# Start of the second expert layer: weights in quarters, residues on GpSimd in halves with a small write behind each

## The chip, the cores and the metric

The kernel runs on one core of one Trainium2 chip. The metric is the device time of one execution in microseconds, as the median of several runs. The engines are named as in the profile: PE is TensorE (matrix products), PEld its weight loads, DVE is VectorE, ACT is ScalarE, POOL is GpSimd, SP is SyncE, whose queue issues most of the DMAs.

## The reference

Three layers follow each other: windowed attention, a mixture of experts with a softmax gate (layer 1), and a second mixture of experts with capacity (layer 2), which this change is about. N = 3072 tokens, D = 512, E = 8 experts, F = 1024.

```python
def _moe2_ref(x, w_gate, w1, w2):
    cap = N // E                                  # 384 tokens for each expert
    logits = x @ w_gate
    order = np.argsort(-logits.flatten())
    for idx in order:                             # greedy: best (token, expert) pair first
        tok, e = idx // E, idx % E
        if assigned[tok] >= 0 or counts[e] >= cap:
            continue
        assigned[tok] = e; counts[e] += 1
    for e in range(E):
        mask = assigned == e
        out[mask] = np.maximum(x[mask] @ w1[e], 0.0) @ w2[e]
```

## The kernel before

**Layer 2 runs expert by expert.** `Ffn.run` walks through 64 steps, 8 chunks of 128 hidden columns for each of the 8 experts. Step s multiplies the first matrix of chunk s (12 matmuls into `ph`, L1013), and then the second matrix of chunk s - LAG (9 matmuls into `y0` to `y2`, L937), with LAG = 2. Every float32 product is made of three: each operand is split into a rounded part h and a residue l, and hh, hl and lh are summed. So each chunk of weights needs two steps of preparation: ACT writes the rounded part (`w1h` L904, `w2h` L886) and another engine subtracts it from the raw weights, which gives the residue (`w1l` L909, `w2l` L890). The same is done to the tokens (`xh`, `xl`) and to the hidden values (`hh` on ACT L1023, `hl` on DVE L1024). The first matrix is split LEAD = 3 steps ahead of its step. The second matrix is split LEAD + LAG = 5 steps ahead of its use (`w2at`). Residues of the first matrix go to DVE for even chunks and to POOL for odd ones, those of the second all to POOL, each as one instruction of 128 x 512.

**Weights** come from HBM in halves of an expert's matrix (`load_half`, 1 MB, two buffers for each matrix). Which expert comes k-th is known only at run time, so SP first loads the number from `em` (written by DVE) or, for the second half, from a copy of it: `em2` for the first expert, copied by DVE in `idle(1)`, and `em3` for the others, copied by POOL behind the gathers.

**Routing** replaces the greedy loop. `Route.steps` finds, for each expert in turn, the threshold at which 384 tokens are at or above it: DVE compares all scores with 64 candidates (`cmp`), PE counts with 13 small matmuls into `rt` (L1658), DVE turns the counts into a flag (`gsm`, `gg`), one matmul spreads it (L1941), and after 3 or 4 such rounds the tokens of the expert are marked in `A`. `compact_steps` turns `A` into three lists of 128 token numbers: it ranks the marked tokens (matmuls L1468, L1473, L1474 and the copy `tb`), builds one-hot rows (`ohb`, `ft` on DVE), multiplies them (28 small matmuls, L1500) and writes `idx`. Then POOL issues three indirect DMAs that gather the tokens into `xg` (L1856), PE transposes them (L788, for the first expert L801) and the next expert can start. The results are written with three indirect DMAs of POOL for each expert (L2018), a `drain` behind the third.

**Order.** Nothing is scheduled by a compiler here (`manual_schedule`): each engine executes what the Python code emits, in that order. `side(q)` is called four times in a step: 0 emits the rounded part of w2, 1 its residue, 2 the rounded part of w1, 3 its residue; between them `src.pop()` and `hook` emit a piece of routing when a simple clock model (`clk`) says that its input is ready. Before the first step of layer 2 there is a stretch with no big matmuls, the first chain: the last rows of layer 1, the routing of the first expert, its weights and its gather. PE is fed with idle products there (`wz` into `y0`, L813), `WT` and `IDLE` say how many, and how many pieces of routing go into the three gaps.

## Time and profile before

| what | value |
|---|---|
| median of 3 runs | 874.37 us (871.49 to 876.87) |
| the profiled execution | 876.25 us, its span 874.5 us |
| PE busy | 831.7 us, 95% of the span |
| DVE, ACT, POOL busy | 610.2, 386.0, 350.4 us |
| layer 2, its first `ph` matmul to the end | from 524.89 us of the span |

The span is the profiled time from the first instruction to the last; 1.75 us of that execution's time lie outside it. Times in rows count from the start of the span. PE is close to full on the whole, so what can be won lies where it waits, where its clock is granted at half, or in work that it need not do.

### The profile page before, as it was taken

What the parts mean: (1) busy time and instruction counts of PE and PEld (TensorE: products, weight loads), DVE (VectorE), ACT (ScalarE), POOL (GpSimd) and SP (SyncE); (2) the same over time, 40 slices, a digit from 0 to 9 for tenths busy, and PEclk for the clock granted to TensorE, in tenths of its full rate; (3) what the DMA queues carried; (4) which work ended last, traced back from release to release, by engine and by line L of the source; (5) the groups of instructions that cost most, each with busy time, mean ns of one, the idle gap of its engine ahead of it and who ended that gap; (6) DMA issues with size and microseconds to landing.
All of it is one profiled execution on the core that took longest, in us unless ns stands there. A gap on an engine that the chain in (4) does not pass through costs nothing.

```text
span 874.5 us, 15223 instructions
## 1 busy us (share of the span) xinstructions
PE 831.7 (95%) x5035; PEld 661.7 (76%) x5040; DVE 610.2 (70%) x1759; ACT 386.0 (44%) x1091; POOL 350.4 (40%) x561
## 2 busy tenths in 40 slices
PE   8889999989999999999999979899999998999996
PEld 4666666667888888888887647787888877789995
DVE  6888787766779696969692587577878585763310
ACT  5667777764443434343423124243434342445431
POOL 5456967654221001010000026436464654475561
PEclk9999999999999999999999979999999999999999
DMA  7434645747354435353349045434433443245201
GB/s 209 162 115 140 147 145 147 243 149 210 95 169 134 156 121 169 120 169 119 123 112 321 13 133 170 157 96 128 174 132 134 133 134 131 91 155 190 97 37 40
DMA packets 70109, 122.85 MB, mean 140 GB/s; under 512 B 9857, under 2 KB 23043, under 8 KB 69894
## 3 DMA queue, kind: packets, MB, share of 16 engines
q1 hardware_dynamic: 63302, 102.36, 37.1%
q0 software_dynamic: 6720, 19.43, 6.9%
q8 instruction: 42, 0.69, 0.3%
q14 instruction: 45, 0.37, 0.2%
HBM read 102.06 MB, written 19.71 MB: 139 GB/s over the span
## 4 chain that ended last, share of the span: by engine, by line
PE 75%; DVE 11%; issue 5%; ACT 4%; DMA 2%; POOL 1%; SPq 0%; POOLq 0%; DVEq 0%; ACTq 0%
PE ph L1013 26%; PE y L937 26%; PE sp L322 4%; PE po L394 3%; ACT P L351 3%; PE tr L788 2%; PE rt L1658 2%; PE pt L359 2%; DVE sc L144 2%; PE px L430 1%; PE rc L1500 1%; PE y L813 1%; PE ph L1285 1%; DVE cmp L144 1%; DVE mx L341 1%
## 5 line engine op out<-in xcount | busy, mean ns | idle before, releaser
L1023 ACT ACTIVATE hh<-ph 128x384 fp32r<-128x384 f32 (+1 forms) x112 | 60.2, 538 | 275.2 <-PE ph L1013 274.6
L1013 PE MATMUL ph<-xh,w1h 128*128 128x384 f32 (+1 forms) x448 | 169.5, 378 | 0.0
L1013 PE MATMUL ph<-xh,w1l 128*128 128x384 f32 (+1 forms) x448 | 162.5, 363 | 1.2 <-DVE w1l L909 1.2
L1013 PE MATMUL ph<-xl,w1h 128*128 128x384 f32 (+1 forms) x448 | 162.0, 363 | 0.0
L937 PE MATMUL y<-w2h,hh 128*128 128x512 f32 x384 | 155.9, 406 | 0.0
L937 PE MATMUL y<-w2l,hh 128*128 128x512 f32 x384 | 151.9, 396 | 0.0
L937 PE MATMUL y<-w2h,hl 128*128 128x512 f32 x384 | 151.9, 395 | 0.0
L1024 DVE SCALAR_TENSOR_TENSOR hl<-ph,hh 128x384 fp32r<-128x384 f32 (+1 forms) x112 | 68.5, 611 | 107.1 <-ACT hh L1023 106.0
L890 POOL TENSOR_TENSOR w2l<-w2r,w2h 128x512 fp32r<-128x512 f32 x64 | 86.4, 1356 | 70.5 <-ACT w2h L886 34.8
L1178 POOL DMA_INDIRECT xg<-xd,ent x26 | 28.7, 1104 | 195.4 <-DMA ent<-idtab 149.6
L1202 DVE SCALAR_TENSOR_TENSOR junk<-yr,wgb 128x512 f32<-128x512 f32 x160 | 103.0, 684 | 0.0
L1013 PEld LDWEIGHTS ph<-xh,w1l 128*128 128x128 f32 x448 | 85.4, 191 | 11.1 <-DVE w1l L909 1.6
L1013 PEld LDWEIGHTS ph<-xh,w1h 128*128 128x128 f32 x448 | 85.7, 191 | 10.1 <-DVE hl L1024 0.2
L351 ACT ACTIVATE P<-sp,mx 128x132 f32<-128x132 f32 x192 | 69.3, 369 | 50.8 <-DVE mx L341 17.5
L1013 PEld LDWEIGHTS ph<-xl,w1h 128*128 128x128 f32 x448 | 85.1, 190 | 7.9 <-DVE xl L804 0.3
L937 PEld LDWEIGHTS y<-w2h,hl 128*128 128x128 f32 x384 | 73.0, 190 | 16.1
L937 PEld LDWEIGHTS y<-w2h,hh 128*128 128x128 f32 x384 | 73.4, 191 | 13.7 <-issue 2.2
L937 PEld LDWEIGHTS y<-w2l,hh 128*128 128x128 f32 x384 | 73.2, 191 | 11.6
L886 ACT ACTIVATE w2h<-w2r 128x512 fp32r<-128x512 f32 x112 | 69.8, 625 | 7.7 <-DMA w2r<-in_w_dram 7.6
L904 ACT ACTIVATE w1h<-w1r 128x512 fp32r<-128x512 f32 x112 | 69.6, 623 | 7.2 <-DMA w1r<-in_w_dram 5.1
L322 PE MATMUL sp<-kr,qs 64*128 64x260 f32 (+1 forms) x384 | 59.0, 406 | 13.2 <-ACT P L351 12.0
L909 DVE TENSOR_TENSOR w1l<-w1r,w1h 128x512 fp32r<-128x512 f32 x80 | 65.9, 824 | 3.0 <-ACT w1h L904 3.0
(391 smaller groups left out, 1398.7 us busy)
## 6 DMA issues: line engine op xcount, KB each, us to landing
w1r<-in_w_dram SPq DMA_DIRECT2D x30, 1024.0 KB, 5.8
w2r<-in_w_dram SPq DMA_DIRECT2D x30, 1024.0 KB, 6.9
vr<-in_v_dram SPq DMA_DIRECT2D x16, 384.0 KB, 4.7
xd<-xb SPq DMA_DIRECT2D x16, 384.0 KB, 3.5
xs<-yr SPq DMA_DIRECT2D x24, 256.0 KB, 6.1
kr<-in_kT_dram SPq DMA_DIRECT2D x15, 396.0 KB, 3.8
qr<-in_qT_dram SPq DMA_DIRECT2D x15, 384.0 KB, 4.2
wgb<-in_wg2T_dram SPq DMA_DIRECT2D x1, 2048.0 KB, 9.2
```

The costliest lines, as they stand in the source:

```text
L322: nc.tensor.matmul(sp[:, hd, c0:260], qs[o:o + 64, 128 * i:128 * i + 128], kr[o:o + 64, k0:k0 + 260 - c0], start=True, stop=True)
L351: nc.scalar.activation(z.P[:, n % 2, hd, :], s.sp[:, hd, 128:260], AF.Exp, bias=s.mx[:, hd:hd + 1], accum_out=z.sm[:, n % 2, hd:hd + 1])
L886: nc.scalar.activation(ch[1][c][0], r[:, q, :], AF.Copy)
L890: eng.tensor_tensor(lo, r[:, q, :], h.bitcast(F32), op=OP.subtract)
L904: nc.scalar.activation(h, v, AF.Copy)
L909: eng.tensor_tensor(lo, v, h.bitcast(F32), op=OP.subtract)
L937: nc.tensor.matmul(o, l, r, start=(first and i == 0), stop=(end and i == 2))
L1013: nc.tensor.matmul(ph, wp[:, c, :], xp_[:, c, 0:NTK], start=(d == 0 and i == 0), stop=(d == 3 and i == len(cut[d]) - 1))
L1023: nc.scalar.activation(hh, ph, AF.Relu)
L1024: nc.vector.scalar_tensor_tensor(hl, ph, 0.0, hh.bitcast(F32), op0=OP.max, op1=OP.subtract)
L1178: self.nc.gpsimd.indirect_dma_start(out=self.xg[j][:, a, :], out_offset=None, in_=self.G.xd[0:k, :], in_offset=bass.IndirectOffsetOnAxis(a ...
L1202: nc.vector.scalar_tensor_tensor(junk, yr[:, 0:DM], 1.0, wgb[:, e, :], op0=OP.mult, op1=OP.mult, accum_out=lg[:, e:e + 1])
```

## The change

1. **First weights in quarters.** For the first expert of layer 2, the first half of each matrix comes as two quarters of 512 KB (`load_quarter`). The second quarters and the second halves are issued after the gathers of the first expert, since SP now reads their expert number from `em3`.
2. **Residues on POOL** are made in two instructions of 256 columns, and behind each stands a MEMSET of one element (`gap`).
3. **First matrix:** of the chunks behind the fourth, all residues are on POOL (before, every second one). DVE keeps chunks 0 and 2.
4. **Second matrix:** from chunk 2 on it is split LAG = 2 steps ahead of its use instead of 5; there are 5 buffers instead of 7.
5. **Ranking:** a scan on DVE (`prefix`) and the row sum that comes with `A` replace two of three ranking matmuls and the copy `tb`; of the one-hot products 26 instead of 28 are left; one reduction replaces a copy and an addition before `idx`, which is now two tiles.
6. **Small things:** the last logits are read from PSUM without a copy; fewer idle products in the first chain; some memsets are made earlier; pieces of routing are emitted in a slightly other order.

```diff
+def load_quarter(nc, pool, w, i, e, k):
+    r = pool.tile([128, 4, 256] if i == 0 else [128, 2, 512], F32, name=("w1q", "w2q")[i])
+    sl = slice(256 * k, 256 * k + 256)
...
-        W2B = LEAD + 2 + (0 if self.vsplit else LAG)
+        W2B = LEAD + 2
...
-            w2at[t - LEAD - (0 if small(c) or self.vsplit else LAG)] = c
+            w2at[t - (LEAD if small(c) or self.vsplit else LAG if c > 1 else LEAD + LAG)] = c
...
+        gap = None if self.vsplit else wk.tile([1, 1], F32, name="gap", bufs=1)
+
+        def residue(eng, o, v, h):
+
+            if eng is nc.vector:
+                eng.tensor_tensor(o, v, h, op=OP.subtract)
+                return
+            n = len(o.shape)
+            for k in range(2):
+                w = slice(256 * k, 256 * k + 256) if n == 2 else slice(2 * k, 2 * k + 2)
+                eng.tensor_tensor(o[:, w], v[:, w], h[:, w], op=OP.subtract)
+                eng.memset(gap, 0.0)
...
-                eng = nc.gpsimd if c % 2 and not self.vsplit else nc.vector
+                eng = nc.gpsimd if (c % 2 or c > 3) and not self.vsplit else nc.vector
...
-            poll_w(1)
+            for i in range(2):
+                if not self.vsplit:
+                    raw[i][0].append(load_quarter(nc, wk, (w1, w2)[i], i, src.ereg2(js[0]), 1))
+                poll_w(1, (i,))
...
-JC, NIT, FEW, IDLE = 64, 4, 2, (2, 2, 1)
+JC, NIT, FEW, IDLE = 64, 4, 2, (3, 2, 1)
...
-    nc.tensor.matmul(cs[:, 0:1], A, o1, start=True, stop=True, skip_group_check=True)
-    tb = p.tile([n, 128], BF, name=tag + "tb", bufs=1)
-    V.tensor_copy(tb, bc(cs[:, 0:1], [n, 128]))
-    warm(wt)
-    yield clk.dve + 0.2
-    nc.tensor.matmul(rk, g.tri, A, start=True, stop=False, skip_group_check=True)
-    nc.tensor.matmul(rk, tb, g.tri[0:n, 0:n], start=False, stop=True, skip_group_check=True)
+    nc.tensor.matmul(bs, g.tri, rs, start=True, stop=True, skip_group_check=True)
...
-    V.scalar_tensor_tensor(r0, rk, 1.0, A, op0=OP.add, op1=OP.mult)
+    V.scalar_tensor_tensor(r0, pre, bs, A, op0=OP.add, op1=OP.mult)
...
+    tiles = [t for t in range(n) if n != NR or t % HR <= HT]
+    for t in tiles:
...
-    V.tensor_copy(pj[:, :, 0:3], dg[:, :, 1])
-    V.scalar_tensor_tensor(pj[:, :, 0:3], dg[:, :, 0], 128.0, pj[:, :, 0:3], op0=OP.mult, op1=OP.add)
+    V.tensor_reduce(pj[:, :, 0:3], acc.rearrange("p (k w a) -> p k a w", w=2, a=3), axis=AX.X, op=OP.add)
...
+def prefix(V, g, p, A, tag):
+
+    n = A.shape[1]
+    t = p.tile([128, n], F32, name=tag + "pre", bufs=3)
+    V.tensor_tensor_scan(t, g.ones[:, 0:n], A, 0.0, op0=OP.mult, op1=OP.add)
+    return t
...
     def ready_e2(self, k):
-        return k == 0 or k in self.em3
+        return k in self.em3
...
-                V.scalar_tensor_tensor(A, S_, lo, oe, op0=OP.is_ge, op1=OP.mult)
+                V.scalar_tensor_tensor(A, S_, lo, oe, op0=OP.is_ge, op1=OP.mult, accum_out=rs)
+                pre = prefix(V, g, p, A, "")
```

What this makes of the engines' programs is seen best at three places. On POOL, in the middle of layer 2, around a gather (`DMA xg` x3) and the copy of the expert's number behind it, before:

```order
L890 TENSOR_TENSOR w2l<-w2r,w2h 128x512
L909 TENSOR_TENSOR w1l<-w1r,w1h 128x512
L890 TENSOR_TENSOR w2l<-w2r,w2h 128x512
L1856 DMA xg_7993<-xs,idx 128x512 x3
L1859 COPY em_7997<-em 1x1
L890 TENSOR_TENSOR w2l<-w2r,w2h 128x512
```

and now, around the gather of the second expert:

```order
L902 TENSOR_TENSOR w2l<-w2r,w2h 128x256
L903 MEMSET gap 1x1
L902 TENSOR_TENSOR w1l<-w1r,w1h 128x256
L903 MEMSET gap 1x1
L902 TENSOR_TENSOR w1l<-w1r,w1h 128x256
L903 MEMSET gap 1x1
L1895 DMA xg_6969<-xs,idx_6965 128x512 x3
L1898 COPY em_6973<-em 1x1
L902 TENSOR_TENSOR w2l<-w2r,w2h 128x256
L903 MEMSET gap 1x1
```

Two residues belong to each step now where one and a half did, and a whole one takes four instructions where it took one.

On SP, from the first load of layer 2's weights on (ISA rows are address work; `em_88` is `em2`, `em_6498` and `em_6961` are `em3`), before:

```order
L768 DMA w1r<-in_w_dram 128x4x512
...
L768 DMA w2r<-in_w_dram 128x4x512
L1831 TENSOR_LOAD em_88
...
L768 DMA w1r<-in_w_dram 128x4x512
...
L768 DMA w2r<-in_w_dram 128x4x512
```

and now:

```order
L767 DMA w1q<-in_w_dram 128x4x256
...
L767 DMA w2q<-in_w_dram 128x2x512
L1870 TENSOR_LOAD em_6498
...
L767 DMA w1q<-in_w_dram 128x4x256
...
L776 DMA w1r<-in_w_dram 128x4x512
...
L767 DMA w2q<-in_w_dram 128x2x512
...
L776 DMA w2r<-in_w_dram 128x4x512
```

The first pair has half the bytes, and everything behind it waits for POOL's copy `em3` in place of DVE's `em2`. (Each of the four later loads has a TENSOR_LOAD of its own ahead of it; one is shown.)

On DVE, in the first steps of the first expert, with the flag `gg` for which PE's next count waits, before:

```order
L1024 SCALAR_TENSOR_TENSOR hl<-ph,hh 128x384 x2
L909 TENSOR_TENSOR w1l<-w1r,w1h 128x512
L144 TENSOR_SCALAR gsm<-rt 64x8
L144 TENSOR_TENSOR gg<-rt,gsm 64x8
L1024 SCALAR_TENSOR_TENSOR hl<-ph,hh 128x384
```

and now:

```order
L1054 SCALAR_TENSOR_TENSOR hl<-ph,hh 128x384
L897 TENSOR_TENSOR w1l<-w1q,w1h 128x512
L1054 SCALAR_TENSOR_TENSOR hl<-ph,hh 128x384
L145 TENSOR_SCALAR gsm<-rt 64x8
L145 TENSOR_TENSOR gg<-rt,gsm 64x8
L1054 SCALAR_TENSOR_TENSOR hl<-ph,hh 128x384
```

The residue ahead of the flag was that of chunk 4 (second half, `w1r`); now it is that of chunk 2 (second quarter, `w1q`), one place earlier, and no residue of w1 stands on DVE behind it.

## Rows read from the trace of the kernel before

**Rows 1.** Engines by stretch; the last three numbers are PEclk, DMA share, GB/s.

```profile
524.80:564.00 39.20, 34.18 (x186) 28.44 (x186) 26.69 (x73) 13.76 (x32) 22.47 (x19) 0.91 0.51 165
...
765.00:851.00 86.00, 86.00 (x462) 77.41 (x462) 33.92 (x55) 38.89 (x78) 55.15 (x56) 1.00 0.36 123
```

**Rows 2.** Waits of PE from 524.8 to 866 us: total, times, longest.

```profile
PE tr L788 <- DMA xg<-xs,idx: 3.5, 4, 1.2
PE tr L788 <- DVE xl L790: 3.3, 3, 1.7
PE rt L1658 <- DVE cmp L144: 2.9, 2, 2.2
PE rt L1941 <- DVE gg L144: 2.1, 1, 2.1
```

**Rows 3.** Stretches of half clock in layer 2, as in rows 1.

```profile
536.40:539.80 3.40, 3.40 (x11) 2.91 (x10) 3.26 (x10) 0.93 (x3) 2.68 (x3) 0.50 0.01 2
```

**Rows 4.** Timeline of the first chain: start, us, engine, instruction [idle before <- releaser].

```profile
511.24 0.19 DVE L144 SCALAR_TENSOR_TENSOR r<-rc,A 128x28 f32<-128x28 f32 x1
...
511.89 0.42 SPq L768 DMA_DIRECT2D w1r<-in_w_dram  x1
...
516.37 0.23 DVE L144 SCALAR_TENSOR_TENSOR idx<-pj 128x3 int32<-128x3 f32 x2
...
520.04 0.95 POOL L1856 DMA_INDIRECT xg<-xs,idx  x1 [0.30 <-issue]
...
523.64 0.33 PE L801 MATMUL tr<-cst,xg 128*128 128x128 f32 x1 [0.56 <-DMA xg<-xs,idx]
```

**Rows 5.** Timeline of the third step of the first expert.

```profile
532.83 0.63 ACT L886 ACTIVATE w2h<-w2r 128x512 fp32r<-128x512 f32 x1 [3.98 <-DMA w2r<-in_w_dram]
...
534.39 0.98 DVE L909 TENSOR_TENSOR w1l<-w1r,w1h 128x512 fp32r<-128x512 f32 x1
...
535.82 0.16 PE L1941 MATMUL rt<-gg,ones 64*128 64x8 bf16 x1 [2.09 <-DVE gg L144]
```

**Rows 6.** The chain of waits at the second expert's one-hot products.

```profile
550.52 1.70 PE rc L1500 x28
```

**Rows 7.** Timeline from the second expert's list to its last transposed block.

```profile
552.73 0.23 DVE L144 SCALAR_TENSOR_TENSOR idx<-pj 128x3 int32<-128x3 f32 x2
...
559.48 0.33 PE L788 MATMUL tr<-cst,xg 128*128 128x128 f32 x1 [1.11 <-DMA xg<-xs,idx]
```

**Rows 8.** DVE forms from 520 to 852 us: xcount, busy us, mean ns, idle before.

```profile
L909 DVE TENSOR_TENSOR w1l<-w1r,w1h 128x512 fp32r<-128x512 f32 x31 | 32.5, 1047 | 2.1 <-ACT w1h L904 2.1
```

**Rows 9.** Timeline of a late DVE residue.

```profile
556.28 2.50 DVE L909 TENSOR_TENSOR w1l<-w1r,w1h 128x512 fp32r<-128x512 f32 x1
```

**Rows 10.** POOL forms of the whole span.

```profile
L890 POOL TENSOR_TENSOR w2l<-w2r,w2h 128x512 fp32r<-128x512 f32 x64 | 86.4, 1356 | 70.5 <-ACT w2h L886 34.8 <-ACT ckm L1933 10.4 <-issue 8.3
...
L404 POOL TENSOR_TENSOR psk<-P,psk 128x16 fp32r<-128x16 f32 x48 | 10.5, 219 | 0.0
...
L2017 POOL MEMSET spacer<- 1x1 f32 x24 | 2.2, 90 | 0.0
```

**Rows 11.** POOL timeline, late experts: a gather, then two scatters.

```profile
790.73 1.00 POOL L1856 DMA_INDIRECT xg<-xs,idx  x1 [0.15 <-issue]
...
794.39 2.56 POOL L890 TENSOR_TENSOR w2l<-w2r,w2h 128x512 fp32r<-128x512 f32 x2
...
803.36 1.02 POOL L2018 DMA_INDIRECT out_dram<-yr,idx  x1 [2.08 <-ACT yr L2016]
...
809.12 1.30 POOL L890 TENSOR_TENSOR w2l<-w2r,w2h 128x512 fp32r<-128x512 f32 x1 [2.15 <-issue]
...
838.25 1.00 POOL L2018 DMA_INDIRECT out_dram<-yr,idx  x1 [2.08 <-ACT yr L2016]
```

**Rows 12.** The chain of waits, one undisturbed step of PE.

```profile
799.64 2.10 PE ph L1013 x12
801.75 2.08 PE y L937 x9
```

More of the change, by code (lines that the diff above doesn't have):

```diff
@@ L853, in load, with poll_w @@
                 e = src.ereg2(alljs[hf // 2]) if hf % 2 else src.ereg(alljs[hf // 2])
-                raw[i][hf] = load_half(nc, self.rawpool, (w1, w2)[i], i, e, hf % 2)
-        def poll_w(n):
+                if hf == 0 and not self.vsplit:
+                    raw[i][hf] = [load_quarter(nc, wk, (w1, w2)[i], i, e, 0)]
+                else:
+                    raw[i][hf] = load_half(nc, self.rawpool, (w1, w2)[i], i, e, hf % 2)
+        def poll_w(n, ws=(0, 1)):
             for _ in range(n):
-                for i in range(2):
+                for i in ws:
                     w = want[i]
@@ L889, in split2 @@
                 eng = nc.vector if self.vsplit or small(c) and c % 2 else nc.gpsimd
-                eng.tensor_tensor(lo, r[:, q, :], h.bitcast(F32), op=OP.subtract)
+                residue(eng, lo, r[q // 2][:, q % 2, :] if isinstance(r, list) else r[:, q, :], h.bitcast(F32))
                 done[1] = c + 1
@@ L896, in split1 @@
                 v = r[:, q, :]
+            elif isinstance(r, list):
+                v = r[q // 2][:, :, 128 * (q % 2):128 * (q % 2) + 128]
             else:
@@ L958, in run @@
             split(-LEAD, 3)
-            ahead = [(s, 2) for s in range(1 - LEAD, 0)] + [(-LEAD, 0), (1 - LEAD, 0)]
+            ahead = [(s, 2) for s in range(1 - LEAD, 0 if self.vsplit else 2 - LEAD)] + [(-LEAD, 0), (1 - LEAD, 0)]
             for s, part in ahead:
@@ L967, in run @@
             for s in range(2 - LEAD, 0):
-                split(s, 0)
-                late.append(s)
+                part = 0 if self.vsplit else 2
+                split(s, part)
+                late.append((s, part + 1))
         clk.pe = max(clk.pe, clk.dve - X0)
@@ L976, in side @@
             def side(q):
+                while q == 3 and late:
+                    split(*late.pop(0))
                 if q == 1 and late:
-                    late.append(s)
+                    late.append((s, 1))
                 else:
                     split(s, q)
-                while q == 3 and late:
-                    split(late.pop(0), 1)
                 if jx + 1 < len(js) and s < total:
@@ L1546, in __init__ @@
         self.cmp = p.tile([128, 2, JC, HR], BF, name="cmp")
+        self.cuts = ((0, HA), (HA, HT + 1))
+        self.cmp2 = [p.tile([128, 2, JC, e - o], BF, name=f"cmp{o}") for o, e in self.cuts]
         self.T = p.tile([128, NR], F32, name="T_")
@@ L1693, in v1 @@
             V.tensor_tensor(Lm, Lm, bc(self.fl[:, None, None, :], [128, 2, HT, E]), op=OP.max)
+            for i in range(SSML):
+                V.tensor_scalar(L[64:128, HR * i + HT], self.fl[64:128], self.pad[64:128, i:i + 1], None, op0=OP.mult)
         def v2():
@@ L2156, in moe2_general @@
             V.copy_predicated(L, mk, neg)
-            idx = compact(nc, g, p, f.ps.tile([128, 512], F32, name="rc"), A, "g")
+            rs = p.tile([128, 1], BF, name="grs")
+            with nc.allow_low_precision("a count of at most NT"):
+                V.tensor_reduce(rs, A, axis=AX.X, op=OP.add)
+            idx = compact(nc, g, p, f.ps.tile([128, 512], F32, name="rc"), A, rs, prefix(V, g, p, A, "g"), "g")[0]
             xg = p.tile([128, 3, DM], F32, name="gxg")
```

93 lines of the change are left out of this document (48 added, 45 removed).

## The prediction

> **What bounds the kernel now.** I read the busy table first: PE is busy for 95% of the span, so only three things can shorten it: PE's waits, stretches at half its clock, and work taken off PE. By stretch [rows 1], 765 to 851 us is full (86.0 of 86.0 us, clock 1.00), while the first expert of layer 2, 524.8 to 564, has 5 us idle and a clock of 0.91. An undisturbed step takes 2.10 + 2.08 us [rows 12], so an expert 33.4 us. 64 steps would be 268 us, but from 524.89 to the last scatter, about 866 us, there are 341: 42.6 for each expert. The list of PE's waits behind 524.8 us [rows 2] holds 11.8 us: 3.5 for gathers, 8.3 for DVE. The clock was granted at 0.50, the lower level (1.2 of 2.4 GHz), in five stretches of 3.3 to 3.4 us with PE busy throughout (one of them is in [rows 3], the others begin at 560.3, 601.2, 717.3 and 734.3); each came just behind PE's waits or a run of small count matmuls, and each costs half its length, 1.7 us, 8.5 together. So at most 20.3 us of layer 2 can be won without removing work. The rest of the difference to 268 us is transposes and routing matmuls, which remain.
>
> **The change part by part.**
>
> *First chain.* The ranking result `r` stands at 511.24 [rows 4]. One small matmul now stands where three and a copy did; against that come a scan and a second accumulator read on DVE. I take 0.6 us off, and 0.3 more for one reduction in place of copy and addition, and for the second `idx` no longer standing ahead of the gather. The list then comes near 515.5 instead of 516.4, the third gather near 519.1 instead of 520.04. The last block landed 3.6 us behind its issue (523.64); that stays, since the 2 MB of weights issued from 511.89 on were not what it waited for. Another 0.2 us come from the logits that aren't copied. Sum: 1.1 us; bounds 0 (DVE's comparison for the second expert falls onto a gather again) and 2.2 (1 MB less traffic helps the gather as well).
>
> *Quarters.* In the third step ACT stood 3.98 us for a half of w2 that was issued 525.26 and landed 532.8; behind it in ACT's order stood `hh` and `w1h`, behind these on DVE a residue at 534.39 and the flag, and PE waited 2.09 us for it [rows 5], then ran 3.4 us at half clock. Now the second pair of loads waits for POOL's copy behind the gathers, near 520 us, instead of DVE's, and the first of them is a quarter, so chunks 2 and 3 should be there near 525 and the halves near 528 and 532, and the residue ahead of the flag is one that needs the quarter alone. On SP nothing but these loads is queued behind the new wait. I take the whole 2.1 us off and the clock stretch with it, 1.7: 3.8. If the quarter is late, the same stall comes back: bound 0.
>
> *PE work.* For each of the seven later experts two small matmuls and two of 28 one-hot products go. The 28 took 1.70 us [rows 6], so two 0.12; a lone small matmul has 0.16 [rows 5]. 7 x (0.12 + 0.32) = 3.1 us as records stand; they overlap, so I take 2.5 and keep 1.5 and 3.1.
>
> *Second expert.* PE waited 2.9 of the 3.5 us here, with the list at 552.73 and the last block transposed at 559.48 [rows 7]. In the new order 9 `ph` matmuls stand behind the one-hot products that stood ahead of them: 1.6 us of work move under the gather. I take 1.0 off the wait and half of the clock stretch behind it: 1.8; bounds 0 and 4.6.
>
> *DVE.* 30 residues leave it. In layer 2 one took 1.05 us on the mean, 31 of them 32.5 us [rows 8], the one at 556.28 2.50 us [rows 9] while POOL ran residues of its own. Others that read two operands from SBUF stretch likewise. DVE's relief costs nothing by itself; it counts where PE waits for it: 3.3 (`xl`) and 2.9 (`cmp`) [rows 2]. I take two thirds, 4.2, and two of the three clock stretches that are left, 3.4. Bounds 0 and 6.2 + 5.1.
>
> A stretched DVE instruction looks like one that stands still until POOL's instruction is over. The Trainium skill (SBUF — State Buffer, Who interferes with whom) says that a DVE instruction with two SBUF inputs contends with a GpSimd instruction that reads SBUF, but not with one that only writes. The trace agrees with the first half (2.50 us for the residue at 556.28); no row here shows the second. By it DVE gets in at the MEMSET behind a half, and the whole 11.3 us of the upper bound would go. If it isn't, a DVE instruction waits for a whole row of halves, and nothing goes.
>
> *POOL.* A residue of 512 columns takes 1.30 us undisturbed [rows 11], a subtraction of 16 columns 0.219, a one-element MEMSET 0.09 [rows 10]. Between the first two a half is 0.219 + 240 x (1.30 - 0.219) / 496 = 0.74 us, so a residue is 2 x (0.74 + 0.09) = 1.66 us; lower bound 1.3 (halves add nothing), upper 2.2 (each half waits some 0.27 us for DVE besides). An expert needs 16 of them, 26.6 us, where it needed 12 and 15.6. The gather holds POOL for 3.7 us (790.73 to 794.39), scatter and drain for 5.8 (803.36 to 809.12) [rows 11]. That is 36.1 us. PE needs 34.9 for a late expert (803.36 to 838.25 [rows 11]) and 40 or more for one with routing. So POOL, half idle before, is nearly full, and just too slow for one late expert. The last one gathers nothing. The second matrix's residue now has two steps, 8.4 us, ahead of its use, instead of five. A scatter and drain of 5.8 us, with the wait for `yr` ahead of it (2.08), takes nearly all of that. I put 1.3 us on this, and 0.5 on fewer idle products ahead of the first step. The gather stands in POOL's queue behind residues that may be late; this is in the bounds of the second expert.
>
> Sum: 1.1 + 3.8 + 2.5 + 1.8 + 4.2 + 3.4 - 1.8 = 15.0 us. Against the profiled execution's 876.25 this is 861.3; that one lies 1.9 us above the median of its three runs, from which the sum gives 859.4. I say 860.
>
> **The rivals.**
>
> *POOL becomes the bound* (slower). Its time for an expert is 16 r + 9.5 us. It reaches the present 42.6 at r = 2.07 and the forecast's 40.7 at r = 1.95. At r = 2.3, if halves mostly wait for DVE, an expert takes 46.3 us and eight 370 instead of 341: 876 + 29 - 7 (first chain, quarters and PE work) = 898; at r = 2.2 it is 885. For it: today's means lie just above the undisturbed time (1356 against 1300 ns [rows 10]) with POOL half idle, and they must rise when it is full. Against: it takes 0.3 us on each residue more than I reckon.
>
> The Trainium skill (GPSIMD Engine Reference, 4.1 Engine selection) says to keep elementwise work on VectorE, GpSimd being about half as fast with two inputs. The trace agrees less strongly, 1.30 us against a mean of 1.05 under contention [rows 8, 11]. By that rule this rival would be the likely case.
>
> *The waits move* (same). The MEMSET lets no DVE instruction in ahead of the next half, or POOL's lateness gives back what DVE gains: 1.1 + 2.1 + 2.5 = 5.7 us remain, less 1.8 for POOL: 872. For it: gathers, DVE and PE wait for each other in turn, and a chain relieved at one end is often held at the next.
>
> *All waits go* (faster). 20.3 + 2.5 + 1.1 = 24 us: 852. For it: DVE has 30 residues less and planned gaps; against: the second expert's gather alone lasts longer than the work laid over it.
>
> **How the numbers follow.** Forecast 0.56, waits move 0.20, all waits go 0.14, POOL bound 0.10. The forecast's own range is 853 to 867. No change means within 1%, 865.6 to 883.1, about what a measurement of this kernel can tell. Faster: 0.14 and nearly all of 0.56, 0.68; same: 0.20 and a rest, 0.23; slower: 0.09. The range leaves out the rival on the slow side and half of the fast one: 850 to 872.
>
> **What would show it.** Right: no wait of PE for the flag in the third step; first `ph` near 523.7; DVE's `ub`, `cmp` and `oc` with no records of more than half a POOL residue above their usual; POOL's busy time in layer 2 near 265 us, halves near 0.75 us. Wrong: PE waiting for `w2l` or `w1l` of POOL at L963 or L1043, above all behind scatters; halves above 0.95 us; half-clock stretches of the same number as now.

## The result, and the profile after

| | median (range), us | against before |
|---|---|---|
| before | 872.88 (867.35 to 876.87), 22 runs | |
| changed | 876.99 (874.89 to 880.91), 22 runs | ratio 1.0055, interval 1.0039 to 1.0072 |

The change makes the kernel 0.55% slower. That is inside the 1% that the prediction called no change, but the interval lies wholly above 1. 860 us was forecast, with 872 as the upper end. The profiled execution has a span of 874.8 us. That of the kernel before, 874.5 us, belongs to an execution 3.4 us above its median, so the two traces end level where the medians differ by 4.1 us.

The first part of the gain arrived. This is the timeline of PE in the changed kernel: start, us, engine, instruction [idle before <- releaser].

```profile
523.21 0.42 PE L1043 MATMUL ph<-xh,w1h 128*128 128x384 f32 x1
...
532.99 0.18 PE L1978 MATMUL rt<-gg,ones 64*128 64x8 bf16 x1
...
609.84 0.34 PE L1043 MATMUL ph<-xh,w1h 128*128 128x384 f32 x1
...
645.97 0.95 PE L1695 MATMUL rt<-OH,cmp 128*128 128x16 bf16 x13 [4.56 <-DVE cmp L145]
...
692.26 0.95 PE L1695 MATMUL rt<-OH,cmp 128*128 128x16 bf16 x13 [5.47 <-DVE cmp L145]
...
705.79 0.33 PE L1043 MATMUL ph<-xh,w1h 128*128 128x384 f32 x1
...
777.95 0.33 PE L1043 MATMUL ph<-xh,w1h 128*128 128x384 f32 x1
```

And this is the same of the kernel before, at the first `ph` of steps 16, 31 and 44 (counted from 0).

```profile
618.99 0.33 PE L1013 MATMUL ph<-xh,w1h 128*128 128x384 f32 x1
...
699.32 0.33 PE L1013 MATMUL ph<-xh,w1h 128*128 128x384 f32 x1
...
777.15 0.34 PE L1013 MATMUL ph<-xh,w1h 128*128 128x384 f32 x1
```

The first step begins at 523.21 instead of 524.89. The flag's matmul at 532.99 comes without the wait of [rows 5]. Step 16 begins at 609.84 instead of 618.99: 9.2 us won. Step 31 begins at 705.79 instead of 699.32: 15.6 us lost in 15 steps. Up to step 44, 5.7 of these are won back (777.95 against 777.15). The two rows between show where the loss is, 4.56 and 5.47 us of idle PE in front of a count. The waits of PE from 524.8 to 866 us are, as in [rows 2] (total, times, longest):

```profile
PE rt L1695 <- DVE cmp L145: 10.0, 2, 5.5
PE tr L796 <- DVE xl L798: 4.4, 3, 2.8
PE rc L2035 <- DVE OH L145: 3.2, 1, 3.2
PE tr L796 <- DMA xg<-xs,idx: 1.5, 2, 0.9
```

PE waits less for gathers (1.5 for 3.5) and hardly for the flag, but 10.0 instead of 2.9 us for `cmp`, and 3.2 for the last check (L2035). By stretch, as in [rows 1], first the lossy one:

```profile
610.00:706.00 96.00, 82.65 (x508) 70.81 (x507) 72.45 (x177) 31.41 (x74) 60.54 (x139) 0.93 0.33 110
...
765.00:851.00 86.00, 86.00 (x461) 77.81 (x460) 16.45 (x34) 39.17 (x79) 69.16 (x177) 1.00 0.42 135
```

The kernel before has hardly any idle PE (80.06 of 80.30 us busy) and no half clock in the same steps, 16 to 31:

```profile
619.00:699.30 80.30, 80.06 (x513) 68.35 (x512) 60.11 (x164) 30.95 (x70) 45.24 (x43) 1.00 0.42 145
```

In and behind the long waits of the changed kernel, the clock was granted at 0.50, the lower of its two levels, in these stretches:

```profile
644.60:651.40 6.80, 5.43 (x28) 5.14 (x29) 2.95 (x8) 1.21 (x3) 0.00 (x0) 0.50 0.02 4
689.00:695.80 6.80, 3.54 (x21) 3.45 (x22) 4.09 (x6) 0.43 (x2) 2.11 (x6) 0.50 0.61 207
743.60:747.00 3.40, 3.40 (x11) 2.91 (x10) 3.30 (x7) 1.70 (x4) 2.54 (x5) 0.50 0.80 301
```

PE was busy for 12.4 us of these 17.0 and idle for the rest, so they cost half of 12.4, 6.2 us, against the 8.5 of the kernel before.

Why `cmp` is late stands on DVE and POOL. The timeline of DVE around the first of the two waits, then at the second:

```profile
637.58 0.18 DVE L145 MAX8 J8m<-rt 128x8 f32<-128x8 f32 x1 [0.90 <-PE rt L1978]
637.79 6.79 DVE L145 SCALAR_TENSOR_TENSOR sc<-J8m,dd,sc 128x1 f32<-128x1 f32 x2
644.50 0.29 DVE L145 TENSOR_SCALAR ub<-S__77,sc,dd 128x28 bf16<-128x28 f32 x1
...
684.54 6.53 DVE L145 TENSOR_SCALAR ub<-S__77,sc,dd 128x28 bf16<-128x28 f32 x1
```

The timeline of POOL over the first:

```profile
637.24 0.72 POOL L902 TENSOR_TENSOR w2l<-w2r,w2h 128x256 fp32r<-128x256 f32 x1
637.91 0.09 POOL L903 MEMSET gap<- 1x1 f32 x1
637.96 0.72 POOL L902 TENSOR_TENSOR w2l<-w2r,w2h 128x256 fp32r<-128x256 f32 x1
...
643.71 0.71 POOL L902 TENSOR_TENSOR w2l<-w2r,w2h 128x256 fp32r<-128x256 f32 x1
644.38 0.09 POOL L903 MEMSET gap<- 1x1 f32 x1
```

Two instructions on 128 single numbers, usually 0.2 us each, take 6.79 us and end with POOL's row of halves (6.66 of it is the first one's). The `ub` at 684.54, usually 0.29 us, takes 6.53. In the first of the two, nine halves and the MEMSETs between them went by. The next half starts 0.05 us after its MEMSET's start (637.96, 637.91), so POOL is never idle between two halves. The halves themselves, as in [rows 10], from 523 to 866 us, are not slow:

```profile
L902 POOL TENSOR_TENSOR w1l<-w1r,w1h 128x256 fp32r<-128x256 f32 x120 | 92.9, 776 | 64.3 <-ACT w1h L930 44.6 <-issue 5.9 <-PE y L963 5.7
L902 POOL TENSOR_TENSOR w2l<-w2r,w2h 128x256 fp32r<-128x256 f32 x120 | 91.0, 759 | 8.7 <-ACT w2h L910 8.6
...
L903 POOL MEMSET gap<- 1x1 f32 x251 | 22.5, 89 | 0.0
```

### The profile page after: what moved, and what is told of

The parts are those of the page before. It is cut to its first block, busy times and chain, and to the rows that moved or that the text cites. A ratio compares the mean times of both kernels' runs of the same rounds, so it can differ in the third digit from the quotient of the medians.

```text
span 874.8 us, 15582 instructions
## 1 busy us (share of the span) xinstructions
PE 820.6 (94%) x5006; PEld 656.5 (75%) x5006; DVE 589.2 (67%) x1730; ACT 385.4 (44%) x1091; POOL 412.1 (47%) x968
## 4 chain that ended last, share of the span: by engine, by line
PE 73%; DVE 16%; ACT 5%; issue 3%; DMA 1%; POOL 1%; DVEq 0%; POOLq 0%; ACTq 0%
PE ph L1043 27%; PE y L963 26%; PE sp L323 4%; PE po L395 3%; ACT P L352 3%; DVE sc L145 2%; PE tr L796 2%; PE rt L1695 2%; PE pt L360 2%; PE rc L1530 1%; DMA xg<-xs,idx 1%; PE px L431 1%; DVE mx L342 1%; DVE cmp L145 1%; DVE ub L145 1%
## 5 line engine op out<-in xcount | busy, mean ns | idle before, releaser
L902 POOL TENSOR_TENSOR w1l<-w1r,w1h 128x256 fp32r<-128x256 f32 x120 | 92.9, 776 | 64.3 <-ACT w1h L930 44.6
L902 POOL TENSOR_TENSOR w2l<-w2r,w2h 128x256 fp32r<-128x256 f32 x120 | 91.0, 759 | 8.7 <-ACT w2h L910 8.6
L323 PE MATMUL sp<-kr,qs 64*128 64x260 f32 (+1 forms) x384 | 59.0, 405 | 13.2 <-ACT P L352 12.0
L930 ACT ACTIVATE w1h<-w1r 128x512 fp32r<-128x512 f32 x108 | 67.4, 624 | 2.3 <-DVE lp L449 2.1
L910 ACT ACTIVATE w2h<-w2r 128x512 fp32r<-128x512 f32 x108 | 67.4, 624 | 0.0
```

Of the source, the lines that this page charges most:

```text
L323: nc.tensor.matmul(sp[:, hd, c0:260], qs[o:o + 64, 128 * i:128 * i + 128], kr[o:o + 64, k0:k0 + 260 - c0], start=True, stop=True)
L902: eng.tensor_tensor(o[:, w], v[:, w], h[:, w], op=OP.subtract)
L910: nc.scalar.activation(ch[1][c][0], r[q // 2][:, q % 2, :] if isinstance(r, list) else r[:, q, :], AF.Copy)
L930: nc.scalar.activation(h, v, AF.Copy)
```

## The experiments

Theory A: the thirty residues moved to POOL make its rows long. Theory B: halves with a tiny write behind each hold DVE, wherever the residues stand. Theory C: the late split of w2 bunches the residues. All edits are to the changed kernel unless another is named; ratios are against before, with their 95% interval. A hold is a record of DVE that is far longer than usual; the lengths given are those of the records. A seam is the place between two instructions of POOL that follow each other.

### Parts of the change undone

**w1_back**

```diff
-                eng = nc.gpsimd if (c % 2 or c > 3) and not self.vsplit else nc.vector
+                eng = nc.gpsimd if c % 2 and not self.vsplit else nc.vector
```

> The changed kernel with the w1 residues divided as before (odd ones on GpSimd, even ones on VectorE); halves, gaps, quarters and first chain stay. Theory A (the thirty residues that moved to GpSimd make its back-to-back rows so long that VectorE, in the middle of routing, is held 6.5 to 6.8 us three times): the rows shorten, no VectorE instruction of layer 2 is held for more than 2.5 us, the idle of PE after 523 us falls from 22 to about 12, the early 9 us stay: 864 to 869 us, ratio to before 0.990 to 0.996. Theory B (halving with a gap is what holds VectorE, wherever the residues stand): the long records stay, VectorE has 20 to 30 us more work besides: 876 to 885. Theory C (the later split of w2 bunches them): 874 to 878, unchanged.

872.38 us, 1.0008 (0.9982 to 1.0033). Two records of `sc` of 6.8 us are still there, with idle PE of 4.7 us behind each, as B said; the time, under B's 876, lies between the two. A alone doesn't explain it. The edit also puts back a charge in the code's clock model, which comes up below.

**whole**

```diff
-            if eng is nc.vector:
+            if eng is nc.vector or len(v.shape) > 0:
                 eng.tensor_tensor(o, v, h, op=OP.subtract)
                 return
```

The condition is always true, so every residue is one instruction, with no write behind it.

> The changed kernel with each residue on GpSimd as one instruction of 512 columns and no gap behind it; the division of the residues, quarters and first chain stay. Theory A (load of GpSimd makes the rows): a residue costs 1.30 to 1.36 us against 2 x 0.76 + gaps, some 0.2 to 0.3 us less, so the rows shorten a little but stay: longest VectorE record 4 to 6 us, 871 to 877 us. Theory B (halves and gaps hold VectorE): the records fall back to the 1.4 to 2.2 us of before and the time to 864 to 869. If the halves do let VectorE in elsewhere, it is over 880.

877.46 us, 1.0054 (1.0027 to 1.0080), with holds of 4.1 to 5.0 us. As A said; B's second half fell: whole residues hold DVE too.

**w1_back_whole**, both edits together.

> The changed kernel with both undone: w1 residues divided as before and whole, no gaps. What is left of the change is the first chain, the quarters and the later split of w2. Theories A and B both: the time before less the 9 us that step 16 shows, 862 to 868 us, ratio 0.988 to 0.995. Theory C (the later split of w2): 870 to 877. If the early 9 us are given back further on by a wait that was there before too, 870 to 873.

870.79 us, 0.9964 (0.9935 to 0.9994). More than A and B said, and within what C, or a gain given back further on, would give. One hold of 5.9 us is left, without a write.

**no_gap**

```diff
-                eng.memset(gap, 0.0)
```

> The changed kernel without the tiny writes; two halves stay for each residue on GpSimd. If a gap lets a waiting VectorE instruction in, the records of VectorE lengthen further (over 7 us) and the time rises above 880. If the gap opens nothing (theory A, the next half starts 0.05 us after the write), GpSimd saves some 0.05 to 0.09 us a half, some 5 us of its busy time in all, the long records of 6 to 7 us stay or get shorter by a tenth, and the time is 874 to 878, no change against the changed kernel.

867.24 us, 0.9946 (0.9918 to 0.9975). 9.8 us less than the changed kernel: neither expectation had it. The same place in the program, timeline of DVE:

```profile
642.10 1.52 DVE L145 SCALAR_TENSOR_TENSOR sc<-J8m,dd,sc 128x1 f32<-128x1 f32 x2
643.55 0.79 DVE L145 TENSOR_SCALAR ub<-S__77,sc,dd 128x28 bf16<-128x28 f32 x1
644.37 1.57 DVE L145 TENSOR_TENSOR cmp<-ub,iou 128x1792 bf16<-128x1792 bf16 x1
```

DVE waits there for the end of a half each time and gets on, though `sc` comes 2.0 us into POOL's row here (from 640.11) as in the changed kernel (from 635.79). Theory D: the write makes DVE lose its turn.

**w1_back_no_gap**, the first edit and this one.

> Halves without the tiny write, and the w1 residues divided as before. It shows what the move of the thirty residues is worth when the write is gone: VectorE has some 30 x 0.85 us of work back, GpSimd 30 x 1.4 us less. Theory D (the write was the fault, the move is good): 868 to 873 us, 1 to 5 us over the 867.2 of the kernel without the write. Theory A (the move was the fault): 861 to 866.

856.80 us, 0.9805 (0.9768 to 0.9841): the fastest kernel of this study, 16 us under before. The move of the residues, too, costs some 10 us.

**w2_earlier_no_gap** (without the write)

```diff
-        W2B = LEAD + 2
+        W2B = LEAD + 2 + (0 if self.vsplit else LAG)
...
-            w2at[t - (LEAD if small(c) or self.vsplit else LAG if c > 1 else LEAD + LAG)] = c
+            w2at[t - (LEAD if small(c) or self.vsplit else LEAD + LAG - 1 if c > 1 else LEAD + LAG)] = c
```

> Halves without the tiny write, and w2's chunks split four steps ahead of their use instead of two (before: five), with two more buffers. Theory C (the later split of w2 puts its residues where they are late): PE's waits for GpSimd's residues and the row behind the gathers shrink, 862 to 866 us. If the later split costs nothing: 866 to 869, as the kernel without the write.

882.02 us, 1.0101 (1.0067 to 1.0135). C fell, and the other way round: the late split is worth 15 us in this order. PE waits 6.4 us for `w1l` of POOL here, and two holds of 6.4 and 5.5 us at `sc` came up, with no write between the halves. So the write isn't needed for a hold.

**wide_gap**

```diff
-        gap = None if self.vsplit else wk.tile([1, 1], F32, name="gap", bufs=1)
+        gap = None if self.vsplit else wk.tile([128, 256], F32, name="gap", bufs=1)
```

> The changed kernel with the write behind each half widened from one element to 128x256. GpSimd has about 250 x 0.1 to 0.3 us = 25 to 75 us more work, still under 500 of 875. If a longer write-only stretch lets VectorE in at every half (which the prediction had of the tiny one), the longest VectorE record on the routing chain falls from 6.7 to under 1.6 us, the three halts of PE of 4.6, 5.5 and 5.4 us and the half clock behind them go: 864 to 869 us, as without the write. If it doesn't, the rows get longer with GpSimd's work: 878 to 890.

899.66 us, 1.0291 (1.0254 to 1.0329). That is above both expectations. Holds of 8.4 and 6.5 us run across writes of 0.30 us each, so a longer write doesn't let DVE in here. GpSimd's own lateness is in this time as well: PE waits 4.6 us for a `w1l` of POOL.

**halves_alone**, the kernel before with the two halves and no write.

```diff
-                eng.tensor_tensor(lo, r[:, q, :], h.bitcast(F32), op=OP.subtract)
+                residue(eng, lo, r[:, q, :], h.bitcast(F32))
...
-                eng.tensor_tensor(lo, v, h.bitcast(F32), op=OP.subtract)
+                residue(eng, lo, v, h.bitcast(F32))
```

> The kernel before, with one edit: each residue on GpSimd is issued as two halves, with no write between them. First chain, loads, the early split of w2 and the division of the residues stay as before. If the halves are what makes the best kernel so far (856.8 us) faster than the same with whole residues (870.8), this takes about as much off the kernel before: 858 to 865 us. If they help only together with the later split of w2 or the quarters, 869 to 874.

874.77 us, 1.0014 (0.9986 to 1.0043): nothing. Halves took 14.0 us off in the new kernel (870.79 to 856.80), but not here, where a DVE residue held for 4.8 us puts a wait of 5.0 in front of the flag's matmul of [rows 5]. That wait was 2.1 before, so it explains only 2.9 us of the 14; the rest stays open.

**quarter_residues**, w1_back_no_gap with four instructions of 128 columns.

> The best kernel so far (no tiny write, w1 residues divided as before, 856.8 us) with each GpSimd residue in four instructions of 128 columns instead of two of 256. If VectorE's wait is the rest of one GpSimd instruction, its usual hold falls from 0.4 to 0.7 us to 0.2 to 0.35, some 10 us of VectorE's time, of which a third to a half stands on the chain: 852 to 856 us. GpSimd's residues cost more, 4 x 0.42 against 2 x 0.73 us. If VectorE misses short seams as it does behind the tiny write, or if GpSimd's time counts: 858 to 870.

873.93 us, 1.0016 (0.9984 to 1.0048), 17 us over the halves and above both expectations: six records of DVE over 2.5 us, the longest of `idx` 11.0 us. Finer isn't better here.

### The order that moved along

In the code stands, beside the choice of the engine, the charge of 0.6 us to the clock model that orders the routing pieces. A residue moved to POOL is not charged, and so routing is emitted earlier.

**no_gap_old_plan** (without the write, residues on POOL)

```diff
-                if eng is nc.vector:
+                if eng is nc.vector or c % 2 == 0:
                     clk.vec(0.6)
```

> Halves without the tiny write, all late w1 residues on GpSimd as in the changed kernel, but the clock by which the code orders the routing steps still adds 0.6 us for each even chunk, as if VectorE did it. Theory F (the move costs 10 us because the order changes: without these 0.6 us the routing's VectorE work is emitted earlier, in front of xl, and TensorE waits 3.4 us for xl): the order is that of the 856.8 us kernel, VectorE has 26 us less to do, and the time is 853 to 860. Theory G (the move costs because GpSimd's queue is full, gathers and residues come later): 864 to 869, as without the write (867.2).

858.42 us, 0.9842 (0.9805 to 0.9879). This is what theory F expected: 8.8 of the 10 us (867.24 to 858.42) come from the order. Without the charge, DVE's timeline in front of expert 4 (no_gap) has the routing ahead of `xl`:

```profile
688.20 0.71 DVE L145 SCALAR_TENSOR_TENSOR sc<-J8m,dd,sc 128x1 f32<-128x1 f32 x1
...
693.19 0.80 DVE L145 TENSOR_TENSOR OH<-L,S__77 128x224 bf16<-128x224 f32 x1
...
695.28 0.55 DVE L798 TENSOR_TENSOR xl<-tr,xh 128x384 fp32r<-128x384 f32 x1
```

and its PE waits for that:

```profile
695.88 0.55 PE L796 MATMUL tr<-cst,xg 128*128 128x128 f32 x3 [3.39 <-DVE xl L798]
```

With the charge (no_gap_old_plan) the two `xl` come first and nobody waits:

```profile
687.25 0.56 DVE L798 TENSOR_TENSOR xl<-tr,xh 128x384 fp32r<-128x384 f32 x1 [1.12 <-ACT xh L797]
...
689.33 0.56 DVE L798 TENSOR_TENSOR xl<-tr,xh 128x384 fp32r<-128x384 f32 x1 [0.47 <-ACT xh L797]
...
690.00 0.32 DVE L145 SCALAR_TENSOR_TENSOR sc<-J8m,dd,sc 128x1 f32<-128x1 f32 x1
```

**w1_back_new_order**, w1_back_no_gap without the charge for chunks behind the fourth.

```diff
-                if eng is nc.vector:
+                if eng is nc.vector and c <= 3:
                     clk.vec(0.6)
```

> The kernel of 856.8 us (no tiny write, w1 residues divided as before), but the clock that orders the routing steps no longer adds 0.6 us for the even late chunks, though VectorE still does them: TensorE's and ScalarE's instructions then stand in the order of the changed kernel, row for row. Theory F (the order costs the 10 us): 866 to 872 us, with TensorE waiting some 3 us for xl and for the last check as without the write (3.4 and 3.1). Theory G (GpSimd's load costs): 855 to 860.

864.42 us, 0.9917 (0.9885 to 0.9950), 7.6 us over the same in the old order, and the wait for `xl` of 3.2 us is back. Somewhat less than F said, but not G.

**tiny_write_old_order**, the changed kernel with the charge of no_gap_old_plan.

> The changed kernel, tiny writes and all, with the one number put back: the clock adds 0.6 us for each even late chunk, so TensorE's instructions stand in the order of before's division. If the write costs the same in every order (9.8 us in the new one, 15.6 with the residues back): 868 to 874 us, with at least two VectorE records of 6 us and more. If the write hurts only where the new order has piled up VectorE's work: 858 to 862.

890.22 us, 1.0215 (1.0185 to 1.0244). Far over both expectations: the write costs 31.8 us here (858.42 without it). With the write in place, the old order alone makes the changed kernel 13.2 us slower, not faster. There are five holds of 4.4 to 11.3 us; PE's waits from 520 to 888 us:

```profile
PE tr L796 <- DVE xl L798: 13.2, 4, 5.0
PE rt L1695 <- DVE cmp L145: 11.0, 3, 5.4
```

**changed_again**, the changed kernel profiled a second time.

> The changed kernel as it is, profiled a second time. If the long holds are bound to places in the program: again sc and ub records of 6 to 7 us in steps 22 and 29 to 30, and PE idle of 4 to 6 us behind them. If they are chance, other places or other lengths, with some 15 to 25 us of PE idle in all since the run's time is steady (874.9 to 880.9).

Holds of 6.7 us at `sc` and 7.3 at `cmp` (usually 1.1), at the same two places of the program (the second one instruction later), and PE idle of 4.58 and 5.47 us behind them (4.56 and 5.47 the first time). In both traces the holds belong to places in the program.

### The holds by themselves

**seams** computes nothing of the reference; in outline:

```python
for r in range(ROW):                 # GpSimd: a row of residues, nothing to wait for
    P.tensor_tensor(lo[:, a], wr[:, a], wh[:, a], op=OP.subtract)   # then, by kind, a write
    P.tensor_tensor(lo[:, b], wr[:, b], wh[:, b], op=OP.subtract)
for it in range(ITER):               # VectorE, with TensorE in between
    V.max(J8, rt[:, 0:8])
    V.scalar_tensor_tensor(sc[:, 0:1], J8[:, 0:1], dd[:, 0:1], sc[:, 1:2], op0=OP.mult, op1=OP.add)
    ...
    V.tensor_tensor(cmp, bc(ub[:, None, :], [128, 64, 28]), bc(iou[:, None, :], [128, 64, 28]), op=OP.is_ge)
```

> A kernel that computes nothing of the reference (all three layers are left out): it measures the disputed cost by itself. In each of 24 phases GpSimd subtracts 24 residues in a row from data that is there already, while VectorE runs nine rounds of the routing step's chain (a maximum out of PSUM, two 128x1 instructions, ub, a comparison of 128x1792, then the count on TensorE). The phases take turns: halves, halves with the tiny write, whole residues, halves with a write of 128x256 behind each, whole ones with the tiny write, VectorE alone. Theory D (the tiny write makes VectorE lose its turn at a seam): with the tiny write some VectorE instructions of 128x1 or 128x28 are held for 3 us and more over several halves, without it none or clearly fewer; the next half starts within 0.06 us of the tiny write. Theory E (the write changes nothing, the three long records of the changed kernel are chance): as many long records with as without. If a write-only stretch lets VectorE in, the phase with the wide write has no record over 1.6 us; if it holds VectorE as a reading one does, long records stand there too.

There is no long hold in any of the 20 rows: the longest wait of a DVE instruction over halves is 0.6 us without the write and 0.8 with it, about the length of one half. The wide writes had been moved out of their place, so that kind said nothing.

**seams_in_order**, the same with the order as written.

> The measurement by itself again, computing nothing of the reference, now with the order on each engine as written (in the run before, the wide writes were moved out of their place), with ScalarE's halves ready before the row and TensorE reading the residues behind it. Thirty phases, six kinds in turn: halves; halves with the tiny write into one element that all share; halves with a tiny write into an element of its own each, so that the write waits for no write before it; halves with the write of 128x256; whole; whole with the tiny write. From the run before: without the write VectorE goes in at the first seam (4 of 95 held instructions missed one), with it 60 of 100 missed one. If the write itself is the fault, its own element changes nothing: over half miss the first seam. If its wait for the write before is the fault, the kind with own elements goes in at the first seam like plain halves. With the wide write: if GpSimd's write-only stretch lets VectorE in, no hold over 0.75 us; if not, as with the tiny one.

| kind (5 rows each) | held over 0.15 us | held on the mean (longest) | from one start to the next |
|---|---|---|---|
| halves | 64 | 0.48 (0.56) us | 0.680 us |
| halves, tiny write | 70 | 0.51 (0.61) | 0.719 |
| halves, tiny write to its own element | 71 | 0.52 (0.61) | 0.719 |
| halves, wide write | 51 | 0.44 (0.82) | 0.933 |
| whole | 47 | 0.96 (1.09) | 1.220 |
| whole, tiny write | 46 | 1.01 (1.13) | 1.257 |

Held is what a record of `sc`, `ub` or `cmp` lasts beyond the shortest of its kind. No wait reaches the time from one start to the next, with the write or without: DVE waits for the rest of one instruction of POOL and gets in. The counts of missed seams in the expectation above (4 of 95 against 60 of 100) don't show otherwise. They hang on 0.04 us: an instruction that starts at a seam stands 0.02 us ahead of the next half in a plain row and 0.06 us behind a write, and then waits for that half in both. If each half that starts during a wait is counted, there are 36 in 64 waits without the write and 39 in 70 with it. So theory D isn't borne out by these rows, and no row of the 30 shows a long hold.

**seams_after_gathers**

> The measurement by itself once more, computing nothing of the reference: each row of 14 residues now follows three gathers of 128 rows and a copy on GpSimd, as in the second layer, and a weight load of 1 MB runs beside it. Kinds: halves, halves with the tiny write, whole; eight phases each. If the gathers make the long holds, VectorE records of 2 us and more stand in the first 10 us behind them; without such records the gathers are not it. The seams should show as before: 3 of 64 missed without the write, over half with it.

All 24 rows held the first 128x1 instruction that came into them to their end, 15.1 to 18.0 us, of each kind alike, with the write or without.

**seams_apart**

> The measurement by itself, computing nothing of the reference, halves without the tiny write only. Seven ways to come into the row, four times each: plain (VectorE's chain starts 2 us behind the row's start), early (it starts with the row), load (plain, with a weight load of 1 MB running), one (plain, one gather ahead of the row), three (three gathers ahead), pause (three gathers, then GpSimd waits some 4 us, then the row), far (the same with a wait of some 15 us). If the gathers make the long holds: plain, early and load get in at the first or second seam (no record over 1 us), one and three hold to the row's end, 14 to 17 us, and pause or far tells whether a rest clears it. If coming late into a running row does it: plain and load hold as well, early does not. If the load does it: load alone.

27 of 28 rows held, plain ones too; the exception is one row behind three gathers. The rows meant to start together with DVE's chain held as well: the first `sc` still came 1.0 us behind the row's start. So it isn't the gathers, the load or a rest. What the rows of the last two runs share is that the first of `sc`, `ub` and `cmp` to meet the row came 1 to 3 us behind its start; in each of the 50 rows of the two runs before, one of them was running when the row began. Later rounds of the chain came into those 50 rows up to 17 us and more behind their start and got in, so coming late is not enough: it is the first meeting with the row that differs.

**seams_breaks**

```diff
                 P.tensor_tensor(lo[:, a], wr[:, a], h[:, a], op=OP.subtract)
+                P.tensor_copy(one[:, 2 * r:2 * r + 1], lo[0:1, e].bitcast(F32))
```

> The measurement by itself, computing nothing of the reference: rows of 28 halves into which VectorE's chain comes 2 to 3 us late, as the rows that held it to their end (16 us). Six kinds, four rows each: plain; a tiny write into an element of its own behind each half; a write of 128x256 behind each half; a one-element copy behind each half that reads the half's last column and so waits until it is done; the same behind each second half; a one-element copy behind each second half that waits for ScalarE to have read the residue. If only an idle GpSimd ends a hold: plain, tiny and wide hold for 14 us and more, the copies that wait let VectorE in within 0.8 us (behind each half) or 1.6 us (behind each second). If the wide write gives way too, the holds of 6 and 8 us in the full kernel with it stay unexplained. If the waits for the own result don't help and the one for ScalarE does, GpSimd's pause has to be longer than some 0.1 us.

The timeline of DVE in a plain row, in one with the wide write and in one with a copy that waits for each half (the edit above):

```profile
14.91 16.23 DVE L154 SCALAR_TENSOR_TENSOR sc<-J8m,dd,sc 128x1 f32<-128x1 f32 x1
...
116.31 0.57 DVE L154 SCALAR_TENSOR_TENSOR sc<-J8m,dd,sc 128x1 f32<-128x1 f32 x1
...
116.94 22.57 DVE L156 TENSOR_SCALAR ub<-S__71,sc,dd 128x28 bf16<-128x28 f32 x1
...
172.82 0.52 DVE L154 SCALAR_TENSOR_TENSOR sc<-J8m,dd,sc 128x1 f32<-128x1 f32 x1
...
173.40 0.88 DVE L156 TENSOR_SCALAR ub<-S__71,sc,dd 128x28 bf16<-128x28 f32 x1
```

Plain, tiny and wide: 12 of 12 rows held an instruction to their end, 16.1 to 22.6 us. The three kinds of copies that wait: none of 12. The timeline of POOL in that last row:

```profile
172.61 0.71 POOL L139 TENSOR_TENSOR lo<-wr,h 128x256 fp32r<-128x256 f32 x1
173.39 0.17 POOL L145 COPY one<-lo 1x1 f32<-1x1 f32 x1
173.53 0.71 POOL L132 TENSOR_TENSOR lo<-wr,h 128x256 fp32r<-128x256 f32 x1
```

The copy starts 0.07 us after the half's end (173.32), while a write starts 0.05 us before it. A half with such a copy takes 0.92 us instead of 0.68. The copies that wait end the holds; that the 0.07 us of rest does it, and not something else about the copy, is argued, not shown. In the full kernel no copy was tried.

## Why the prediction was wrong, point by point

The failed step is the term for DVE: waits less 4.2 us and clock less 3.4. Waits for `cmp`, `xl` and the last check rose from 6.2 to 17.6 us. Of three stretches of half clock, 5.1 us, the term was to remove two; three remained and cost 6.2. The prediction let DVE in at the MEMSET behind a half and named its own alternative: otherwise a DVE instruction waits for a whole row. That is what happened, at two places, 6.7 and 6.5 us long. Two things stand behind the loss. The first is shown by taking it away alone, the second only where the first is gone:

- **The write.** Its removal is worth 9.8 us in the changed kernel (876.99 to 867.24), 15.6 with the residues back (872.38 to 856.80), 31.8 in the old order (890.22 to 858.42), and in all three pairs the holds of 4.4 us and more go with it. How the write does this isn't shown. In rows by themselves no wait is much longer with it than one half (0.8 us at most) where DVE is there when the row begins, and where DVE comes late the row holds with the write or without. In one kernel holds of 6.4 and 5.5 us came without it (w2_earlier_no_gap). The write also spaces the halves differently (0.72 us instead of 0.68), and that this alone shifts where DVE meets them was not ruled out.
- **The order**, once the write is gone. The prediction had no term for it. The charge to the clock model went with the residues, and routing slid ahead of `xl`: 8.8 us with the residues on POOL (867.24 to 858.42), 7.6 with them on DVE (864.42 to 856.80). The move by itself costs 1.6 to 2.8 us, within the intervals no difference, though DVE has 30 residues less to do.

The write and the order don't add up: with the write, the new order is the better one (876.99 against 890.22). That the order also decides where DVE meets a row would explain this, but isn't shown.

The Trainium skill (SBUF — State Buffer, Who interferes with whom) says that whoever issues first gets the ports that DVE and GpSimd share for the whole instruction while the other blocks, and that a DVE instruction with two inputs from SBUF contends with a GpSimd instruction that reads SBUF, not with one that only writes. The runs agree with the contention (6.66 us for `sc` at 637.79), and with the second point for `sc` (0.57 us in the wide row). A wait for one instruction is all that the page speaks of, and here the runs differ: `ub` at 116.94 let 24 halves go by that started after it.

The other terms:

- *First chain*, 1.1: the first `ph` came 1.7 us earlier (523.21 for 524.89). Right in size, but by luck: 1.6 us of it were there when the last product of layer 1 ended (495.82 for 497.40). Ahead of it, the kernel before was granted the lower clock, 0.50 for 3.4 us from 481.8, and the changed one was not; the prediction has no term for that. From that product to the list `idx`, where ranking, reduction and logits were to give 1.1, it is 18.82 us instead of 18.97.
- *Quarters, second expert, PE work*: from the first `ph` to that of step 9, 47.1 us instead of 53.0, so 5.9 less; the terms give 3.8 + 1.8 and 0.4 of PE work up to there, 6.0. Right: 2.0 us of it are idle PE (5.7 to 3.7 us), 3.4 the two stretches of half clock. The wait for the flag is gone, and no half clock is granted from 518.3 to 644.6.
- *POOL*: 0.74 us for a half was forecast, 0.76 to 0.78 is the mean of records. But the MEMSETs lie over the halves: from one start to the next it is 0.72 to 0.73 us, so a residue takes 1.45 and not 1.66. 265 us of POOL in layer 2 were forecast, 242 measured. PE waited for none of its residues, so the 1.3 us that the sum put on their lateness were not there. The rival with POOL as the bound was rightly put low, and two steps' lead for w2 are enough (an earlier split costs 15 us).
- *All terms together* without write and with the old charge: 858.42 us against the forecast's 860. The sum was about right for that kernel, but its terms aren't shown by that. With the thirty residues back on DVE it takes 856.80, so the relief of DVE by their move won nothing that can be measured, while halving them won 14.0 us (870.79 to 856.80).

The rival "the waits move" (872) came nearest, and its mechanism is the one seen; its price was too low, since it let the waits stay as they were.

What stays open: why a DVE instruction sometimes gets in at the next seam of a running row and sometimes not until its end. In the measurements the first meeting with a row goes along with it: 63 of the 64 rows without a waiting copy held, where it came 1 to 3 us late, and none of the 50 where DVE was there when the row began. The first hold of the changed kernel fits (row from 635.79, `sc` at 637.79), the second doesn't: an `sc` was under way when its row began at 683.86. And in the full kernel many instructions that come late do get in, as `sc` at 642.10 of no_gap, 2.0 us into a plain row behind gathers; by themselves all eight such rows of seams_after_gathers held. That the holds are gone in the two best kernels but for one of 3.0 us is shown; why just there is not.

## What to carry to other kernels

Before work is moved from one engine to another, look for what else hangs on the choice: here a line of bookkeeping reordered a whole layer, for more than the move was worth. Before counting on a pause made for another engine, look for it in the trace (start of the next minus end of the last): here there was none, and only a copy that had to wait let VectorE in. Compare waits by their length and not by a count of missed gaps, which can hang on some hundredths of a microsecond. And undo the parts of a change singly and in pairs: several parts here were good, and the sum was slower than before.

## What the hardware showed that I had not expected

- A VectorE instruction of 128x1 or 128x28 waited up to 22.6 us behind GpSimd's row of ready two-input subtractions, and each time to the row's end, in 63 measured rows. A write-only instruction between them, of 0.09 or 0.31 us, didn't end it. A one-element copy that waits for the half before it (0.07 us of idle GpSimd) did, in 12 of 12 rows.
- A tiny write overlaps the end of the half ahead of it and the start of the next (0.719 us from start to start instead of 0.680), and where VectorE is there when the row begins, it hardly waits longer for that: 0.61 us at most against 0.56 without the write, in the rows of seams_in_order.
- Halves of residues are worth 10 to 14 us where whole ones hold VectorE (877.46 to 867.24, 870.79 to 856.80), quarters lose it again (873.93). In the kernel before, halves are worth nothing (874.77).
